# Middle tiles of an attention and MoE kernel: another order of the first layer's products, and q's main part turned right behind x

## The chip, the cores and the metric

The kernel runs on one core of a Trainium2 chip. A core has a matrix engine (PE, with its weight loads shown as PEld), a vector engine (DVE), a scalar engine (ACT), GpSimd (POOL), a queue engine for transfers (SP), and 16 DMA engines. Each engine works through its own list of instructions; engines wait for one another through semaphores. The metric is the device time of one execution in microseconds, as a median of several runs; lower is better.

## What is computed

```python
kv  = np.einsum('bhsd,bhse->bhde', k, v)
out = np.einsum('bhsd,bhde->bhse', q, kv)
rms = np.sqrt(np.mean(out * out, axis=-1, keepdims=True) + 1e-06)
out = out / rms * g_norm
x = out.transpose(0, 2, 1, 3).reshape(B * S, H * D)
h = x @ w_in
g = h * (1.0 / (1.0 + np.exp(-1.702 * h)))
return g @ w_out
```

There are 8 batches with 8 heads, 576 rows and a head size of 64; x is 4608 x 512, w_in is 512 x 2048 and w_out is 2048 x 512. The output is float32. The kernel computes in float16 with float32 sums.

## The kernel before

**Tiles.** Of each batch's 576 rows, 512 make one tile (t = 0 to 7) and the 64 that remain are gathered from all batches into a ninth (t = 8). A tile passes through two layers. While a tile t is in its second layer, the attention of batch b = t + 1 runs between its matmuls, so that the next tile's x is ready when the first layer of t + 1 begins.

**Products.** From t = 1 on both layers use a seven-product scheme (Strassen's, in Winograd's form): a 2 x 2 block product takes seven block products and some sums. In the first layer (class `SevenIn`) the 16 column blocks of w_in form four parts, g = 0 to 3, each with seven products, p = 1 to 7. A step such as "25" is product 5 of part 2: four matmuls of 128 x 256. Products 1 and 2 take their moving operand from the first column half of x (the blocks b11 and b21); product 3 takes b22; products 5, 6, 7 and 4 take the sums t0, t1, t2 and t3, which DVE forms from x (`Sums.form`, L505 to L509). form(0) is b12 - b11 and form(1) is b22 + t0, so both need the second column half of x.

**Evacuation of a product.** Each part has banks x, y and z in PSUM. Product 1 goes to x; bank x is then copied to y (`copy(self.snap[1], ...)`, L587), and product 6 accumulates on x. Product 5 goes to z, and z is copied to the SBUF tile s5 (L589). When both 5 and 6 are done, DVE writes x + s5 into z (L591), on which product 3 then accumulates. Product 2 accumulates on y. Behind product 7 DVE adds x into s5 (L593). Products 2, 3, 4 and 7 return a gate: an ACT activation (L557) that writes gT. `hid_seven` (L733) walks the steps; the gate of a step is emitted behind the product, and the copy, of the next step. A step's number is its place in the list, and the dictionaries of the plan name such places.

**The plan.** `LATER` (L941) is used for t = 2 to 6. In it `{1: 'DAAA', 5: 'AAAD'}` gives, for parts 0 to 3, the engine of the copy behind product 1 and behind product 5: D is DVE and A is ACT. The string "aooa" gives the pools of the banks x, "aahh" those of z; y is always in h. Pool o has two buffers, which the second layer uses too: its bank z, then its bank x, whose last content is copied out by ACT at the tile's end (`place`, L677). `(0, 1, 5, 10)` are the steps behind which form(0) to form(3) are emitted. `{15: '34'}` puts one product behind matmul 15 of the second layer.

**The second layer and the attention in it.** `Seven.run` (L687) makes 112 matmuls in the order of products 1, 5, 6, 2, 7, 3, 4. Work put there by `at2(n, ...)` is emitted behind matmul n. The attention's `rows` come at 15, and `turn` at 35, 38, 46 and 48. A turn with an odd number issues on SP a DMA_TRANSPOSE (L365) of half of the normalised rows x16 into x, so at 38 the first and at 48 the second column half. The store of the first output half (L843) is issued behind matmul 95, the second at the end.

**Queues of transfers.** At 100 comes `transpose_q` of batch t + 2 (t = 1 to 5): two DMA_TRANSPOSE on SP, the main part into qTd (L289, one buffer, read by the next tile's `rows`) and the remaining rows into qTr (L291). SP's list in a tile is thus x's two halves, the first store, q's main part, q's rest, the second store. On POOL stand, in this order, the k load of batch t + 3 (at 15, behind the products that read k), a mark that waits for x (`after_turn`, L127), the v load and both remainders, a mark that waits for qTd (`after_queries`, L131), and the q load of batch t + 3 (L143, L149).

Of the kernel before, what the change touches and what calls it, by code (L numbers as in the profile page):

```python
# [16 lines left out]
def kernel(  # L17
# [119 lines left out]
    def q_rows(b):  # L137

        rows = qbuf if b % 2 else qraw.rearrange("p c x -> p (c x)")
        return rows[:, 0 : H * J * D]  # L140
# [79 lines left out]
    class Attention:  # L220
# [66 lines left out]
        def transpose_q(self):  # L287
            self.qTd = attn.tile([P, H * J // 2, P], F16, name="qTd", tag="qTd", bufs=1)
            nc.sync.dma_start_transpose(out=self.qTd, in_=q_rows(self.b))  # L289
            self.qTr = attn.tile([P, 2, P], F16, name="qTr", tag="qTr", bufs=1)  # L290
            nc.sync.dma_start_transpose(  # L291
                out=self.qTr, in_=qrem[self.b % 2].rearrange("p c e -> p (c e)")
            )
# [4 lines left out]
        def product(self, t, c):  # L298
            nc.tensor.matmul(t, self.kb[:, c, :], self.qT[c][:, 0:SM], start=True, stop=True)  # L299
# [226 lines left out]
    def copy(engine, to, src):  # L526
        (nc.vector.tensor_copy if engine == "D" else nc.scalar.copy)(to, src)  # L527

    class SevenIn:


        def __init__(self, hid, xs, g, todo):
            self.snap = {p: e[g] for p, e in todo.snap.items()}
            self.pool = todo.pool[g]
            self.gT, self.xs, self.g, self.i = hid.gT, xs, g, PARTS[g]
            self.bank, self.done = {}, set()
            self.s5 = stage.tile([P, 2, TH], F32, name="s5", tag="s5")
# [28 lines left out]
        def product(self, p):  # L566

            name = {1: "x", 6: "x", 7: "x", 4: "x", 2: "y", 5: "z", 3: "z"}[p]  # L570
            if p in (1, 5):
                self.open(name)
            bank = self.bank
            for a in range(2):
                for k in range(KH):
                    w, x = self.operands(p, a, k)
                    nc.tensor.matmul(  # L577
                        bank[name][:, a],
                        w,
                        x,  # L580
                        start=(p in (1, 5) and a == 0 and k == 0),
                        stop=(k == KH - 1),
                        skip_group_check=True,
                    )
            self.done.add(p)
            if p == 1:
                copy(self.snap[1], self.open("y"), bank["x"])  # L587
            elif p == 5:
                copy(self.snap[5], self.s5, bank["z"])  # L589
            if p in (5, 6) and self.done >= {5, 6}:  # L590
                nc.vector.tensor_add(bank["z"], bank["x"], self.s5)  # L591
            elif p == 7:
                nc.vector.tensor_add(self.s5, bank["x"], self.s5)  # L593
                return lambda: self.gate(1, 1, self.s5)
            elif p in (2, 3, 4):
                r, n = {2: (0, 0), 3: (0, 1), 4: (1, 0)}[p]
                return lambda: self.gate(r, n, bank[name])
# [312 lines left out]
    for fo in COLS[4:GROUP]:  # L910
# [28 lines left out]
        {'rows': (19, 19), 'add_up': (22, 26, 27, 31), 'table': 26, 'roots': (27, 33), 'turn': (40, 50, 51, 52)},  # L939
    )  # L940
    LATER = Plan(  # L941
# [4 lines left out]
        {1: 'DAAA', 5: 'AAAD'},  # L946
        "D",
        "aooa",
        "aahh",
        {15: '34'},  # L950
        (0, 1, 5, 10),
        {'rows': (15, 15), 'add_up': (17, 20, 24, 28), 'table': 24, 'roots': (28, 29), 'turn': (35, 38, 46, 48)},
    )
    LAST_TWO = Plan(
# [12 lines left out]
    def plan(t):  # L967
        return SECOND if t < EARLY else LATER if t < B - 1 else LAST_TWO
# [7 lines left out]
    for t in range(NT):  # L976
        b = t + 1
        u1, u2 = {}, {}

        def at1(i, f, *args):  # L980
            u1.setdefault(i, []).append(lambda: f(*args))

        def at2(i, f, *args):
            u2.setdefault(i, []).append(lambda: f(*args))  # L984

        def of(b, name, *args):
            return lambda: getattr(live[b], name)(*args)

        if t == 0:
            for l in range(2):  # L990
                at1(6, nc.vector.memset, kvd[l], 0.0)
            at1(7, of(0, "out", NPAIR))
            at1(7, scale_w_in, 0, 4)
            at1(7, w_in_sums, 0, 2)
            at1(8, start, 1)
            at1(12, scale_w_in, 4, 6)
            at1(12, w_in_sums, 2, 3)
            at1(13, load_q, 2)
            at2(4, setattr, a0, "ss_pool", Attention.ss_pool)
            at2(4, of(0, "ss", NPAIR, True))  # L1000
            at2(4, of(0, "apply", NPAIR))
            at2(18, weight_sum, 0, 0, HF)
            at2(18, scale_w_in, 6, 8)
            at2(18, w_in_sums, 3, 4)
            for c in range(NPAIR):
                at1(12, of(1, "pack_q", c))
                at2(9 + 3 * c, of(1, "q", c))
                at2((36, 36, 49, 49)[c], of(1, "kv", c))
                at2((41, 43, 54, 55)[c], of(1, "out", c))
                at2((45, 50, 58, 60)[c], of(1, "ss", c))  # L1010
                at2((48, 52, 58, 62)[c], of(1, "apply", c))
            for n in range(1, 4):
                at2(19, weight_sum, n, 0, 4)
                at2(38, weight_sum, n, 4, 6)
            at2(39, load_kv, 2, 0, H // 2, False)
            at2(51, clear_rest)
            at2(51, load_kv, 2, H // 2, H)

            def first_sum():
                made[1] = Sums(1, xT[1])  # L1020
                made[1].form(0)

            at2(55, first_sum)
        elif b < B:
            todo = plan(t)
            at = todo.attn
            if t == 1:
                at1(todo.steps.index("kv"), of(b, "kv_all", "D"))
                at1(5, start, b)
                at1(5, of(b, "transpose_q"))  # L1030
                at1(4, nc.scalar.preload_act_table_set, "gelu_apprx_sigmoid_and_others")
                for n, i in ((1, 8), (2, 11), (3, 16)):
                    at1(i, weight_sum, n, 6, HF)
                at1(22, load_kv, 3)
                at1(22, load_q, 3)
                at2(88, start, 3)
                at2(88, of(3, "kv_all", "A"))
                at2(89, load_kv, 4)
                at2(89, load_q, 4)
            elif t + 2 < B:  # L1040
                at2(at["rows"][0], start, t + 2)
                at2(at["rows"][0], of(t + 2, "kv_products"))
                at2(52, of(t + 2, "kv_copies", "A"))
                if t + 3 < B:
                    at2(at["rows"][0], load_kv, t + 3, 0, H, False, "k")
                    at2(101, after_turn, b)
                    at2(101, load_kv, t + 3, 0, H, True, "v")
                    at2(101, after_queries, t + 2)
                    at2(101, load_q, t + 3)
            if t + 2 < B:  # L1050
                at2(100, of(t + 2, "transpose_q"))
            at2(at["table"], nc.scalar.preload_act_table_set, "abs_reciprocal_sqrt_and_small")
            for h in range(2):
                at2(at["roots"][h], of(b, "roots", h))
            for j in range(J):
                if j < J // 2:
                    at2(at["rows"][j], of(b, "rows", j))
                for name in ("add_up", "turn"):
                    at2(at[name][j], of(b, name, j))
            rest = (80, 90, 96, 97) if 1 < t < B - 2 else (46, 74, 80, 82)  # L1060
            at2(rest[0], of(b, "out", NPAIR))
            at2(rest[1], of(b, "ss", NPAIR))
            at2(rest[2], of(b, "apply", NPAIR))
            at2(rest[3], nc.scalar.preload_act_table_set, "gelu_apprx_sigmoid_and_others")
        elif t < B:
            for name in ("ss_pool", "rest_pool"):
                at2(16, setattr, live[1], name, (ps_a, "att"))
            at2(16, of(1, "out", NPAIR))
            at2(34, nc.scalar.preload_act_table_set, "abs_reciprocal_sqrt_and_small")
            at2(44, of(1, "ss", NPAIR))  # L1070
            at2(50, of(1, "apply", NPAIR))
            at2(52, nc.scalar.preload_act_table_set, "gelu_apprx_sigmoid_and_others")
        layers(t, u1, u2)
# [30 lines left out]
```

## Time and profile before

| what | value |
|---|---|
| median of 3 runs | 258.92 us (258.73 to 259.25) |
| the profiled execution's own time | 259.85 us |
| its span, first to last instruction | 258.1 us |
| PE's granted clock | 1.000 |
| start of the first layer's matmuls of t = 2, 3, 4, 5, 6, 7 (us in the span) | 74.04, 100.25, 126.37, 153.60, 179.72, 205.10 |

In the profile a row of the timeline gives start and length in us, the engine, the line of the kernel, the operation, its tiles (output <- inputs), the count of merged instructions, and in brackets the idle time before it with what ended that. "h" stands for a bank of the first layer, "s" for s5, "o" for a bank of the second layer, "xS" for a formed sum. A row of waits gives the total in us, the number of waits, and the longest. A row of stretches gives the window, its length, each engine's busy time with its count of instructions (PE, PEld, DVE, ACT, POOL), PE's clock, the DMA share and GB/s. Matmuls overlap: a row's length reaches to the modelled end of its last one, so the rate is read from start to start.

### The profile page before, as it was taken

Reading aid. Unit: us, or ns where it says so; the run is one execution under the profiler, and the core shown is the slowest. Engines: PE = TensorE matmul, PEld = TensorE weight load, DVE = VectorE, ACT = ScalarE, POOL = GpSimd, SP = SyncE. Lnnn points to the kernel's source line nnn. Section 1 sums busy time; section 2 is a strip of 40 time slices with the busy share of each in tenths; the row PEclk is TensorE's granted clock in tenths of the full one; section 3 lists DMA queues with packets and bytes.
Section 4 is the critical chain, followed back from the end, with each engine's and each line's share of the span. In section 5 each row is a group of like instructions: output and inputs, shape, how many; then the busy total and the mean of one; then the engine's idle time right before and its main releaser. Section 6 shows DMA issues by size and latency. Waiting matters only on the chain.

```text
span 258.1 us, 6355 instructions
## 1 busy us (share of the span) xinstructions
PE 250.8 (97%) x2596; PEld 204.0 (79%) x2596; DVE 190.1 (74%) x339; ACT 180.2 (70%) x327; POOL 57.2 (22%) x91
## 2 busy tenths in 40 slices
PE   8889999999999999999899999999999999999994
PEld 2444554788888888888788888898888888888883
DVE  1565677899938794889469867986799787857872
ACT  3477725988769886988589958995899469536800
POOL 8872235116080103041160130200000000000013
PEclk9999999999999999999999999999999999999999
DMA  7999999999999986999999669986700430012005
GB/s 173 193 200 205 204 204 197 234 198 150 159 178 201 203 118 139 139 136 169 182 144 205 82 152 134 156 95 137 204 3 0 84 163 3 0 60 105 3 19 145
DMA packets 68671, 35.33 MB, mean 137 GB/s; under 512 B 37954, under 2 KB 66242, under 8 KB 68386
## 3 DMA queue, kind: packets, MB, share of 16 engines
q0 software_dynamic: 37616, 18.31, 55.6%
q1 hardware_dynamic: 30624, 16.29, 29.5%
q8 instruction: 20, 0.33, 0.5%
q10 hardware_dynamic: 402, 0.33, 0.4%
q14 instruction: 9, 0.07, 0.1%
HBM read 36.70 MB, written 9.44 MB: 179 GB/s over the span
## 4 chain that ended last, share of the span: by engine, by line
PE 89%; DMA 7%; DVE 1%; issue 0%; ACT 0%; POOL 0%; DVEq 0%
PE h L577 38%; PE o L697 36%; PE o L812 5%; PE hT L470 5%; DMA xT<-x 2%; DMA vbuf<-in_v_dram 2%; DMA qraw<-in_q_dram 2%; PE kvp L246 2%; PE outR L329 1%; PE ss L376 1%; DVE x L359 1%; PE outT L299 0%; PE q L451 0%; PE kvp L258 0%; DVE xT L386 0%
## 5 line engine op out<-in xcount | busy, mean ns | idle before, releaser
L557 ACT ACTIVATE gT<-h 128x512 f16<-128x512 f32 x96 | 52.3, 601 | 5.6 <-PE h L577 5.6
L577 PEld LDWEIGHTS <-ws 128*128 128x128 f16 x512 | 50.1, 98 | 7.0 <-issue 1.1
L577 PE MATMUL h<-xS,ws 128*128 128x256 f16 x384 | 53.0, 273 | 1.0 <-DVE xS L509 1.0
L697 PEld LDWEIGHTS <-gS 128*128 128x128 f16 x512 | 49.0, 98 | 6.2 <-DVE gS L629 0.3
L697 PE MATMUL o<-tw,gS 128*128 128x256 f16 x384 | 45.6, 273 | 0.0
L577 PEld LDWEIGHTS <-w_in_sb 128*128 128x128 f16 x384 | 37.5, 98 | 4.7
L697 PEld LDWEIGHTS <-gT 128*128 128x128 f16 x384 | 37.6, 98 | 4.3
L577 PE MATMUL h<-xT,w_in_sb 128*128 128x256 f16 x224 | 31.8, 273 | 0.0
L697 PE MATMUL o<-w_out_sb,gT 128*128 128x256 f16 x256 | 31.4, 273 | 0.0
L591 DVE TENSOR_TENSOR h<-h,s 128x512 f32<-128x512 f32 x32 | 22.3, 699 | 11.3 <-PE h L577 5.3
L674 DVE TENSOR_TENSOR osb<-o,qf 128x512 f32<-128x512 f32 (+1 forms) x25 | 16.7, 668 | 11.7 <-PE o L697 11.7
L593 DVE TENSOR_TENSOR s<-h,s 128x512 f32<-128x512 f32 x32 | 22.1, 691 | 4.4 <-PE h L577 3.3
L629 DVE TENSOR_TENSOR gS<-gT 128x512 f16<-128x512 f16 (+2 forms) x32 | 21.3, 685 | 0.6 <-ACT gT L557 0.6
L557 ACT ACTIVATE gT<-s 128x512 f16<-128x512 f32 x32 | 19.8, 628 | 2.6 <-DVE s L593 2.6
L731 POOL DMA_DIRECT2D out_dram<-osb x6 | 3.2, 540 | 82.5 <-DVE osb L674 82.5
L577 PE MATMUL h<-xS,w_in_sb 128*128 128x256 f16 x128 | 18.9, 272 | 0.0
L345 DVE TENSOR_REDUCE sum<-sq 128x8 f32<-128x512 f16 x24 | 14.9, 678 | 4.8 <-ACT sq L339 4.8
L984 ACT ACT_TABLE_LOAD x14 | 18.0, 1283 | 0.3
L317 ACT ACTIVATE sq<-outT 128x512 f16<-128x512 f32 (+1 forms) x16 | 7.8, 489 | 14.5 <-PE outT L299 8.9
L378 ACT ACTIVATE rs<-ss,eps_t 128x512 f32<-128x512 f32 (+1 forms) x16 | 9.2, 581 | 11.5 <-PE ss L376 11.4
L527 ACT COPY h<-h 128x512 f32<-128x512 f32 x27 | 15.4, 577 | 2.2 <-PE h L577 2.0
L577 PE MATMUL h<-xT,ws 128*128 128x256 f16 x112 | 16.8, 273 | 0.0
(104 smaller groups left out, 358.9 us busy)
## 6 DMA issues: line engine op xcount, KB each, us to landing
out_dram<-osb SPq DMA_DIRECT2D x8, 512.0 KB, 4.3
kraw<-in_k_dram POOLq DMA_DIRECT2D x5, 512.0 KB, 7.4
vbuf<-in_v_dram POOLq DMA_DIRECT2D x5, 512.0 KB, 10.2
out_dram<-osb SPq DMA_DIRECT2D x2, 1024.0 KB, 4.8
qraw<-in_q_dram POOLq DMA_DIRECT2D x3, 512.0 KB, 12.2
qbuf<-in_q_dram POOLq DMA_DIRECT2D x3, 512.0 KB, 6.0
out_dram<-osb SPq DMA_DIRECT2D x6, 192.0 KB, 5.7
w_in_sb<-in_moe_w_in_dram POOLq DMA_DIRECT2D x2, 512.0 KB, 9.8
```

Of the source, the lines that this page charges most:

```text
L345: nc.vector.tensor_reduce(out=self.sum4[:, j, :], in_=self.o[j][1].rearrange("p (x d) -> p x d", d=D), op=ALU.add, axis=mybir.AxisListType.X,)
L470: nc.tensor.matmul(self.h[fo], w_in_sb[:, ko, fo * P : (fo + 1) * P], self.x[:, ko], start=(ko == 0), stop=(ko == KO - 1),)
L527: (nc.vector.tensor_copy if engine == "D" else nc.scalar.copy)(to, src)
L557: nc.scalar.activation(self.gT[:, to, n * TH : (n + 1) * TH], src, AFT.Gelu_apprx_sigmoid)
L577: nc.tensor.matmul(bank[name][:, a], w, x, start=(p in (1, 5) and a == 0 and k == 0), stop=(k == KH - 1), skip_group_check=True,)
L591: nc.vector.tensor_add(bank["z"], bank["x"], self.s5)
L593: nc.vector.tensor_add(self.s5, bank["x"], self.s5)
L629: op(s[:, n, lo], a, b)
L674: nc.vector.tensor_add(o, ps, self.kept[with_][:, m])
L697: nc.tensor.matmul(o, a, w, start=(p in (1, 2, 5) and i == 0 and (mo == 0 or split)), stop=(i == HF - 1), skip_group_check=True,)
L812: nc.tensor.matmul(os[mo], gT[:, fo, mo * P : (mo + 1) * P], w_out_sb[:, fo, :], start=(fo == 0), stop=(fo == FO - 1),)
L984: u2.setdefault(i, []).append(lambda: f(*args))
```

## The change

In `LATER` the step "11" moves from the seventh to the third place, "22" and "25" change places, and a new step "10" stands behind "06". A part that has such a step "g0" is held: its product 1 is not followed by the copy of bank x into y, and the copy is emitted at step "10". form(0) and form(1) are both emitted behind step 0; the other numbers move by one with the longer list. `transpose_q` is split: q's main part is issued at matmul 49 of the second layer, directly behind x's second half, for t = 2 to 5 (at 100 as before for t = 1), and q's rest stays at 100.

```diff
         def transpose_q(self):
             self.qTd = attn.tile([P, H * J // 2, P], F16, name="qTd", tag="qTd", bufs=1)
             nc.sync.dma_start_transpose(out=self.qTd, in_=q_rows(self.b))
+
+        def transpose_rest(self):
             self.qTr = attn.tile([P, 2, P], F16, name="qTr", tag="qTr", bufs=1)
...
             self.snap = {p: e[g] for p, e in todo.snap.items()}
+            self.held = f"{g}0" in todo.steps
...
+            bank = self.bank
+            if p == 0:
+                copy(self.snap[1], self.open("y"), bank["x"])
+                return None
             name = {1: "x", 6: "x", 7: "x", 4: "x", 2: "y", 5: "z", 3: "z"}[p]
             if p in (1, 5):
                 self.open(name)
-            bank = self.bank
...
-            if p == 1:
+            if p == 1 and not self.held:
                 copy(self.snap[1], self.open("y"), bank["x"])
...
     LATER = Plan(
-        "21 01 25 22 05 06 11 02 15 26 03 16 12"
+        "21 01 11 22 25 05 06 10 02 15 26 03 16 12"
         " 07 31 27 13 17 35 36 04 23 24 32 33 14 37",
-        {22: ((0, 4, 0), (0, 4, 1)), 25: ((4, 6, 0),)},
+        {23: ((0, 4, 0), (0, 4, 1)), 26: ((4, 6, 0),)},
...
-        (0, 1, 5, 10),
+        (0, 0, 6, 11),
...
                 at1(5, of(b, "transpose_q"))
+                at1(5, of(b, "transpose_rest"))
...
             if t + 2 < B:
-                at2(100, of(t + 2, "transpose_q"))
+                at2(49 if t > 1 else 100, of(t + 2, "transpose_q"))
+                at2(100, of(t + 2, "transpose_rest"))
```

## The prediction

> **What bounds the kernel now.** I read the page first, then the chain of waits, then PE's waits, then a table of time by tile.
>
> ```profile
> span 258.1 us, 6355 instructions
> PE 250.8 (97%) x2596; PEld 204.0 (79%) x2596; DVE 190.1 (74%) x339; ACT 180.2 (70%) x327; POOL 57.2 (22%) x91
> ...
> PE 89%; DMA 7%; DVE 1%; issue 0%; ACT 0%; POOL 0%; DVEq 0%
> ```
>
> PE is 97% busy and 89% of the chain that ended last. So a change of order can gain only where PE stands idle. From the second tile on, PE's waits show one such place:
>
> ```profile
> PE h L577 <- DVE xS L509: 1.0, 1, 1.0
> ```
>
> The table of stretches, cut at the first L577 matmul of tiles t=4, 5 and 6, gives the price of that wait:
>
> ```profile
> 126.37:153.60 27.23, 26.27 (x303) 23.27 (x301) 20.66 (x35) 21.17 (x40) 6.92 (x11) 1.00 0.96 146
> 153.60:179.72 26.12, 26.12 (x303) 23.27 (x301) 20.33 (x34) 21.17 (x40) 3.72 (x7) 1.00 0.95 133
> ```
>
> Both tiles have 303 matmuls at clock 1.00; the fourth is 27.23 - 26.12 = 1.11 us longer. This is all that the change can win on PE. The timeline there (PE, then DVE, then SP's queue) shows why:
>
> ```profile
> 126.37 1.04 PE L577 MATMUL h<-xT,w_in_sb 128*128 128x256 f16 x8
> 128.37 0.60 PE L577 MATMUL h<-xS,ws 128*128 128x256 f16 x4 [0.96 <-DVE xS L509]
> ```
> ```profile
> 127.89 0.42 DVE L509 TENSOR_TENSOR xS<-xT 128x512 f16<-128x512 f16 x1 [2.04 <-DMA xT<-x]
> ```
> ```profile
> 120.56 3.70 SPq L365 DMA_TRANSPOSE xT<-x  x2
> ```
>
> Products 21 and 01 run, then 25 needs form(0), and form(0) needs x's second turned half, which landed late. DMA issues in the two stretches 120-124 and 142-150 us show how late: 5.9 us to landing, against 3.2 us one tile on.
>
> ```profile
> xT<-x SPq DMA_TRANSPOSE x2, 5.9
> ```
> ```profile
> xT<-x SPq DMA_TRANSPOSE x2, 3.2
> ```
>
> **The change, part by part.** No instruction is added or taken away. Three orders change in tiles t=2 to 6 (plan LATER): PE's products, with them ACT's and DVE's queues, and SP's queue.
>
> *Products.* I use the undisturbed tile t=5, which starts at 153.60. PE:
>
> ```profile
> 153.60 1.04 PE L577 MATMUL h<-xT,w_in_sb 128*128 128x256 f16 x8
> 154.47 0.60 PE L577 MATMUL h<-xS,ws 128*128 128x256 f16 x4
> 154.93 0.60 PE L577 MATMUL h<-xT,w_in_sb 128*128 128x256 f16 x4
> 155.36 1.04 PE L577 MATMUL h<-xS,ws 128*128 128x256 f16 x8
> 156.23 1.04 PE L577 MATMUL h<-xT,w_in_sb 128*128 128x256 f16 x8
> 157.11 1.04 PE L577 MATMUL h<-xS,ws 128*128 128x256 f16 x8
> 157.98 0.60 PE L577 MATMUL h<-xT,ws 128*128 128x256 f16 x4
> ```
>
> Four matmuls are a product. The rows are 21 and 01; 25; 22; 05 and 06; 11 and 02; 15 and 26; 03. The eleventh product (03) starts 4.38 us after the first, so a product takes 0.438 us. ACT and DVE beside it:
>
> ```profile
> 153.80 0.58 ACT L677 COPY osb<-o 128x512 f32<-128x512 f32 x1 [0.52 <-PE o L697]
> 154.28 0.59 ACT L527 COPY h<-h 128x512 f32<-128x512 f32 x1
> 155.11 0.58 ACT L527 COPY s<-h 128x512 f32<-128x512 f32 x1 [0.24 <-PE h L577]
> 156.00 0.58 ACT L527 COPY s<-h 128x512 f32<-128x512 f32 x1 [0.30 <-PE h L577]
> 156.48 0.60 ACT L557 ACTIVATE gT<-h 128x512 f16<-128x512 f32 x1
> 157.12 0.57 ACT L527 COPY h<-h 128x512 f32<-128x512 f32 x1
> ```
> ```profile
> 153.00 0.42 DVE L509 TENSOR_TENSOR xS<-xT 128x512 f16<-128x512 f16 x1
> 154.68 0.70 DVE L527 COPY h<-h 128x512 f32<-128x512 f32 x1 [1.26 <-PE h L577]
> 155.28 0.41 DVE L509 TENSOR_TENSOR xS<-xT,xS 128x512 f16<-128x512 f16 x1
> 156.61 0.70 DVE L591 TENSOR_TENSOR h<-h,s 128x512 f32<-128x512 f32 x1 [0.92 <-ACT s L527]
> ```
>
> ACT's rows are: the previous tile's last output copy; 21's copy; 25's copy to s5; 05's copy to s5; 22's gate; 11's copy. DVE's are form(0), 01's copy, form(1), and the add behind 06 (L591), which writes bank z of part 0. Product 03 accumulates into that bank, so it waits for this add, and the add for 05's copy.
>
> Durations: from a product's start to its copy 0.64 (154.47 to 155.11, 155.36 to 156.00); on ACT copy to gate 0.48 (156.00 to 156.48), gate to copy 0.64 (156.48 to 157.12; 11 had started at 156.23 and was ready at 156.87, so the engine set this); end of 05's copy to the add 0.03 (156.58 to 156.61); end of a DVE result to PE 0.06 (127.89 + 0.42 to 128.37).
>
> Before: the add ends at 157.31, so z is ready at 157.37, 0.61 us ahead of 03.
>
> After: 25 is the fifth product and no longer the third. It starts at 153.60 + 4 x 0.438 = 155.35, its copy at 155.99. The gate of 22, now one step ahead of 25, is queued right behind 25's copy and **ahead** of 05's copy (a step's gate is called behind the next step's product): 156.47. Then 05's copy 157.11 to 157.69, the add 157.72 to 158.42, z ready 158.48. 03 is still the eleventh product and wanted at 157.98: **PE waits 0.50 us.** 05's copy starts 1.11 us later than before (157.11 against 156.00); 0.61 of that was slack. ACT meanwhile stands idle between 154.87 and 155.99.
>
> The ACT row itself bears on this order: 22 started at 154.93, ready at 155.57, and ACT stood idle for 0.30 us before 156.00, yet the gate ran behind 05's copy. The Trainium skill's "PSUM — Partial Sum Buffer", section Engine vs sequencer instructions, says that ScalarE's and VectorE's queues are strictly first in, first out; the trace agrees with this 0.30 us. By that rule the wait is the 0.50; without it, with ACT free to choose, it would be gone.
>
> How often: all five tiles have this same chain. The waits of DVE in 74 to 206 us:
>
> ```profile
> DVE h L591 <- ACT s L527: 4.9, 5, 1.2
> ```
>
> Five waits, one a tile: +2.50 us. Bounds: if a copy can follow a gate after 0.48, 0.34 a tile; if each ACT instruction runs serially (0.58 + 0.60 in place of 0.48 + 0.64), and product 11, now third, waits 0.10 besides, 0.66 a tile. Product 11 takes the bank that the output copy at 153.80 frees at 154.38; with 0.06 that is 154.44 against a start at 154.48, so I take nothing for it. The range for five is 1.7 to 3.3, and I take 2.50 since each term is a row of the same tile. Behind 03 everything only shifts; PE is dense there and nothing takes the 0.50 back.
>
> *The forms.* form(0) and form(1) now both come ahead of 01's copy. With x in time they run at 153.00 to 153.83, before that copy is ready (154.68): nothing. 06 needs 01's copy (ends 155.38) at 156.23: covered. 11's copy, held back two products, lands behind 05's on ACT at 157.59 to 158.16; 16, wanted at 158.42, is covered.
>
> *q's main part.* Its DMA_TRANSPOSE moves ahead of the first store on SP, in t=2 to 5:
>
> ```profile
> 152.77 0.33 SPq L843 DMA_DIRECT2D out_dram<-osb  x1
> 153.28 5.50 SPq L289 DMA_TRANSPOSE qTd<-qraw  x1
> ```
>
> The store goes later by up to those 5.5 us. Its output tile has two buffers and is refilled two tiles on, so nobody waits. qTd is read in the next tile's rows, 15 us on. On POOL the mark for qTd stands ahead of the q load, the remainder loads and the next k load:
>
> ```profile
> 152.31 0.18 POOL L127 COPY mark<-xT 1x1 f16<-1x1 f16 x1 [8.76 <-DMA xT<-x]
> ...
> 154.31 0.70 POOL L120 DMA_DIRECT2D vbuf<-in_v_dram  x1
> 165.71 0.18 POOL L131 COPY mark<-qTd 1x1 f16<-1x1 f16 x1 [10.70 <-DMA qTd<-qraw]
> ```
>
> It waited 10.70 us; now q's load follows the v loads nearly at once. In t=3 the same wait had pushed the q load to 114.06, and the k load queues behind it:
>
> ```profile
> 114.06 0.89 POOL L143 DMA_DIRECT2D qbuf<-in_q_dram  x1
> ```
>
> These two ran into x's transposition at 120.56, the late one. With q loaded several us sooner, I take the 3.2 us landing there: -1.11 us (bounds 0 and -1.11). The Trainium skill's "DMA: Bandwidth & Descriptors", section Queues, rings and completion order, has each DMA engine alternate between queue rows packet by packet, and consume one ring in order. By it POOL's loads slow x and q's transposition behind x does not; the 5.9 against 3.2 us agrees, and the sum would be the same.
>
> The earlier q load stands behind v in POOL's queue. v's last piece and its reader:
>
> ```profile
> vbuf<-in_v_dram POOLq DMA_DIRECT2D x1, 64.0 KB, 11.1
> ```
> ```profile
> 167.68 0.82 PE L246 MATMUL kvp<-vbuf,kraw 128*64 128x64 f16 x40
> ```
>
> 154.31 + 11.1 = 165.4: 2.3 us of cover. I cost it at nothing; without that cover PE waits the excess.
>
> *Sum.* +2.50 - 1.11 = +1.39 us. The profiled execution took 259.85 us (span 258.1 and 1.75 around it), giving 261.24. The median of the runs, 258.92, is 0.93 lower, so 258.92 + 1.39 = **260.3 us**.
>
> **The rivals.**
> (a) *Only the gain.* 05's copy reaches DVE early enough that 03 doesn't wait, and x's stall goes: 258.92 - 1.11 = 257.8, faster. It decides at a copy start of 156.61 or sooner, 0.50 ahead of my 157.11. For it: ACT is only 70% busy. Against it: its queue order, and the same chain in five tiles.
> (b) *Nothing to win.* In unprofiled runs, 0.93 us shorter, x may land in time already. Then only the waits remain: 258.92 + 2.50 = 261.4.
> (c) *x stays late* in t=3 (landing 127.8, form(0) 127.89): 25 starts at 128.37 against 128.12, and 03 is 0.75 us late in all against 1.11 before. Four tiles at 0.50 and -0.36: +1.64, 260.6.
> (d) *q's transposition slows x.* If the two share the engines and 3.2 us doubles, x lands at 152.31 + 3.2 = 155.5; form(0) and 0.06 more make 25 start at 156.0, 0.65 late, which adds to the 0.50. Four tiles: +2.6, 262.9. It decides only from a landing after 154.87, 2.5 us later than now; x standing ahead in the same queue speaks against it.
> (e) *The waits are short* (0.2 a tile): +1.0 - 1.11, no change, 258.8.
>
> **How the numbers follow.** My forecast 0.64, (a) 0.13, (b) 0.12, (c) 0.03, (d) 0.03, (e) 0.05. A measurement here tells 0.2%, 0.5 us, from no change. The forecast's own range is 1.7 to 3.3 less 1.11: 259.5 to 261.1. With (b) and (c) and the runs' spread (258.73 to 259.25) the range is 259.3 to 261.6, leaving out (a), (d) and (e), 0.21. Slower 0.82, within 0.05, faster 0.13.
>
> **What would show it.** Right: PE h L577 waits five times, some 0.5 us each, for DVE h L591; its wait for xS is gone; 22's gate stands between 25's and 05's copies on ACT; POOL's mark for qTd waits far less than 10 us, and x lands in about 3.2 us in t=3. Wrong: no wait of PE at 03 (a), five tiles of equal length as before but one shorter; or waits for xS or kvp that weren't there (d).

## The result, and the profile after

| | before | after |
|---|---|---|
| median | 259.25 us (11 runs, 258.73 to 260.3) | 260.51 us (11 runs, 260.11 to 262.3) |
| ratio after / before | | 1.0063, 95% interval 1.0047 to 1.0079 |
| span of the profiled execution | 258.1 us | 258.4 us |

The changed kernel is slower by some 0.5 to 0.8%. The prediction was 260.3 us, in a range of 259.3 to 261.6. The two profiled spans are much closer together than the medians. That has a reason, which the experiments give: the profiled execution of before holds a wait that a second profile of the same kernel doesn't have.

The lines of the changed kernel are shifted: L509 is now L511, L527 is L529, L557 is L560, L577 is L583, L591 is L597, L674 is L680, L677 is L683, L697 is L703. Its page, the span, PE's row and the chain:

```profile
span 258.4 us, 6349 instructions
...
PE 250.2 (97%) x2596; PEld 203.5 (79%) x2596; DVE 190.2 (74%) x339; ACT 179.0 (69%) x327; POOL 56.6 (22%) x91
...
PE 88%; DMA 4%; ACT 3%; DVE 2%; issue 0%; POOL 0%
```

ACT and DVE have entered the chain with 3% and 2%. PE's waits (total, times, longest) name where:

```profile
PE h L583 <- DVE h L597: 1.0, 5, 0.2
```

These are five waits for the add behind 06, one a tile; the wait for the formed sum xS is gone. The 1.0 us understates the loss, since this view counts from the modelled end of the last matmul and not from the next start. The stretches of t = 2 to 6, each from its first matmul to that of the next tile, give it (window, length, then the engines' busy times):

```profile
73.79:100.28 26.49, 26.29 (x304) 23.27 (x302) 20.09 (x34) 20.94 (x40) 4.92 (x8) 1.00 1.13 170
100.28:126.76 26.48, 26.28 (x303) 23.26 (x301) 20.34 (x35) 20.93 (x40) 5.18 (x10) 1.00 1.00 149
126.76:153.25 26.49, 26.29 (x304) 23.27 (x301) 20.35 (x35) 20.93 (x40) 5.92 (x10) 1.00 1.03 152
153.25:179.74 26.49, 26.29 (x304) 23.25 (x302) 20.11 (x34) 20.93 (x40) 3.90 (x7) 1.00 0.92 127
179.74:205.47 25.73, 25.53 (x264) 22.53 (x261) 21.05 (x37) 19.36 (x36) 0.00 (x0) 1.00 0.31 75
```

The first four take 26.48 or 26.49 us where an undisturbed tile of before took 26.12: 0.37 us a tile. The fifth, t = 6, has fewer matmuls and takes 25.73 us against 25.37 in the second profile of before. In all this is 1.83 us. The timelines of ACT, DVE and PE at the start of t = 5, now at 153.25:

```profile
153.93 0.59 ACT L529 COPY h<-h 128x512 f32<-128x512 f32 x1
155.65 0.58 ACT L529 COPY s<-h 128x512 f32<-128x512 f32 x1 [1.12 <-PE h L583]
156.13 0.60 ACT L560 ACTIVATE gT<-h 128x512 f16<-128x512 f32 x1
156.62 0.59 ACT L529 COPY s<-h 128x512 f32<-128x512 f32 x1
157.08 0.62 ACT L529 COPY h<-h 128x512 f32<-128x512 f32 x1
```
```profile
157.24 0.70 DVE L597 TENSOR_TENSOR h<-h,s 128x512 f32<-128x512 f32 x1 [2.22 <-ACT s L529]
```
```profile
156.75 1.04 PE L583 MATMUL h<-xS,ws 128*128 128x256 f16 x8
157.99 0.60 PE L583 MATMUL h<-xT,ws 128*128 128x256 f16 x4 [0.20 <-DVE h L597]
```

ACT's order is 21's copy, 25's copy, 22's gate, 05's copy, 11's copy. It idles 1.12 us before 25's copy, the gate takes its turn, and 05's copy starts 3.37 us into the tile (156.62 - 153.25), where it was 2.40 before (156.00 - 153.60). DVE's add waits 2.22 us for it. Product 03 starts at 157.99 in place of 156.75 + 8 x 0.109 = 157.62.

q's main part goes as the change says. SP's queue and POOL's mark for qTd in the same tile turn:

```profile
147.43 2.61 SPq L367 DMA_TRANSPOSE xT<-x  x2
150.22 1.88 SPq L289 DMA_TRANSPOSE qTd<-qraw  x1
152.42 0.76 SPq L849 DMA_DIRECT2D out_dram<-osb  x1
```
```profile
154.84 0.18 POOL L131 COPY mark<-qTd 1x1 f16<-1x1 f16 x1
155.11 0.89 POOL L143 DMA_DIRECT2D qbuf<-in_q_dram  x1
```

The mark no longer waits, and q's load is issued at 155.11 where it was at 166.16.

### The profile page after: what moved, and what is told of

It reads as the page before. It is cut to its first block, busy times and chain, and to the rows that moved or that the text cites. A ratio compares the mean times of both kernels' runs of the same rounds, so it can differ in the third digit from the quotient of the medians.

```text
span 258.4 us, 6349 instructions
## 1 busy us (share of the span) xinstructions
PE 250.2 (97%) x2596; PEld 203.5 (79%) x2596; DVE 190.2 (74%) x339; ACT 179.0 (69%) x327; POOL 56.6 (22%) x91
## 4 chain that ended last, share of the span: by engine, by line
PE 88%; DMA 4%; ACT 3%; DVE 2%; issue 0%; POOL 0%
PE o L703 38%; PE h L583 34%; PE o L818 5%; PE hT L472 5%; DMA vbuf<-in_v_dram 2%; ACT s L529 2%; DMA qraw<-in_q_dram 2%; PE kvp L246 2%; DVE h L597 1%; PE outR L331 1%; ACT gT L560 1%; PE ss L378 1%; PE outT L301 0%; PE q L453 0%; PE kvp L258 0%
## 5 line engine op out<-in xcount | busy, mean ns | idle before, releaser
L560 ACT ACTIVATE gT<-h 128x512 f16<-128x512 f32 x96 | 52.6, 602 | 6.2 <-PE h L583 6.2
L583 PEld LDWEIGHTS <-ws 128*128 128x128 f16 x512 | 50.0, 98 | 7.7 <-issue 1.9
L703 PEld LDWEIGHTS <-gS 128*128 128x128 f16 x512 | 49.0, 98 | 6.2 <-DVE gS L635 0.3
L583 PE MATMUL h<-xS,ws 128*128 128x256 f16 x384 | 52.2, 273 | 0.0
L703 PE MATMUL o<-tw,gS 128*128 128x256 f16 x384 | 45.6, 273 | 0.0
L583 PEld LDWEIGHTS <-w_in_sb 128*128 128x128 f16 x384 | 37.4, 98 | 4.8
L703 PEld LDWEIGHTS <-gT 128*128 128x128 f16 x384 | 37.6, 98 | 4.3
L597 DVE TENSOR_TENSOR h<-h,s 128x512 f32<-128x512 f32 x32 | 22.2, 697 | 14.8 <-ACT s L529 11.1
L703 PE MATMUL o<-w_out_sb,gT 128*128 128x256 f16 x256 | 31.4, 273 | 0.0
L583 PE MATMUL h<-xT,w_in_sb 128*128 128x256 f16 x224 | 31.1, 273 | 0.0
L680 DVE TENSOR_TENSOR osb<-o,qf 128x512 f32<-128x512 f32 (+1 forms) x25 | 16.7, 668 | 11.8 <-PE o L703 11.7
L560 ACT ACTIVATE gT<-s 128x512 f16<-128x512 f32 x32 | 19.9, 628 | 2.6 <-DVE s L599 2.6
L583 PE MATMUL h<-xS,w_in_sb 128*128 128x256 f16 x128 | 18.9, 273 | 0.0
L115 POOL DMA_DIRECT2D kraw<-in_k_dram x7 | 6.0, 853 | 57.9 <-PE kvp L246 53.6
L583 PE MATMUL h<-xT,ws 128*128 128x256 f16 x112 | 16.8, 272 | 1.0 <-DVE h L597 1.0
```

Of the source, the lines that this page charges most:

```text
L560: nc.scalar.activation(self.gT[:, to, n * TH : (n + 1) * TH], src, AFT.Gelu_apprx_sigmoid)
L583: nc.tensor.matmul(bank[name][:, a], w, x, start=(p in (1, 5) and a == 0 and k == 0), stop=(k == KH - 1), skip_group_check=True,)
L680: nc.vector.tensor_add(o, ps, self.kept[with_][:, m])
L703: nc.tensor.matmul(o, a, w, start=(p in (1, 2, 5) and i == 0 and (mo == 0 or split)), stop=(i == HF - 1), skip_group_check=True,)
```

## The experiments

Theory 1 was that the loss is product 03's wait behind ACT's queue. The rivals were the moved transposition, DVE's own queue, and another wait under the same name. Medians of before beside each experiment: 258.93 us (35 runs) for the first four, 259.07 and 259.15 (13 runs each) for the later ones.

**The order alone.** q's main part goes back to matmul 100.

```diff
-                at2(49 if t > 1 else 100, of(t + 2, "transpose_q"))
+                at2(100, of(t + 2, "transpose_q"))
```

> The new product order alone; q's main part is turned at matmul 100 again, behind the first store. Theory 1 (the loss is product 03's wait for the add behind ACT's queue): five waits of PE for DVE's add, 0.37 us each from start to start as in the changed kernel (1.83 us in all); in t=3 x's second half may land late as before, and then 25 starts 0.25 us late and 03 about 0.6 us late in all. Time 260.5 to 261.0 us. Theory 2 (the moved transposition costs the time, by the store or POOL's queue behind it): no slower than before, 259.3 or less.

Measured: 260.66 us, ratio 1.0060 (1.0038 to 1.0081). All five waits are there at full size:

```profile
PE h L583 <- DVE h L597: 1.0, 5, 0.2
```

The x of t = 3 landed in 3.95 us and cost nothing. The order alone gives the whole loss.

**q alone.** The plan's steps, ready and sums as before, with the transposition at 49.

```diff
-        "21 01 11 22 25 05 06 10 02 15 26 03 16 12"
+        "21 01 25 22 05 06 11 02 15 26 03 16 12"
...
-        (0, 0, 6, 11),
+        (0, 1, 5, 10),
```

> q's main part turned right behind x alone; the old product order. Theory 1: no wait of PE for DVE's add; no wait for form(0), since q's load no longer stands in front of the k load when x is turned in t=3 (x lands in about 3.2 us, the tile takes 26.12 us and not 27.23): 258.3 to 258.8 us against 259.25 before. Theory 2: slower than before, about 260.5. Rival 3 (the late x is chance and not q's load): the wait for form(0) is there in some tile, about 259.3.

Measured: 259.04 us, ratio 1.0007 (0.9983 to 1.0032). So the move costs nothing, but it doesn't win what was expected either; of the three expectations rival 3 came nearest. x's second half took 4.9 us in t = 3, though q's load had long been done; PE lost 0.08 us there (the tile took 26.20 us). So x can be late in t = 3 without q's load.

**05's copy on DVE.**

```diff
-        {1: 'DAAA', 5: 'AAAD'},
+        {1: 'DAAA', 5: 'DAAD'},
```

> The changed kernel with the copy behind product 05 on DVE in place of ACT, so that it isn't queued behind 22's gate. Theory 1: the copy starts 2.84 us into the tile on DVE, the add 3.45, z is ready at 4.2, before product 03 at 4.38: no wait of PE there, 1.83 us less than the changed kernel, 258.5 to 258.9 us. A rival (DVE itself is full there, by both forms ahead of the copies): PE still waits about 0.3 us in each of five tiles, 260.2 or more.

Measured: 259.06 us, ratio 0.9997 (0.9975 to 1.0018). No wait of PE for the add is left, and the tiles t = 2 to 5 take 26.12 or 26.13 us each. So DVE is not the limit. The time is that of before and not below it.

**22's gate one step later.** ACT's work is unchanged, and two instructions change places.

```diff
             behind, gates = gates, []
+            if step == "25" and "10" in todo.steps:
+                behind, gates = [], behind
```

> The changed kernel with 22's gate called one step later, behind 05's copy on ACT; nothing else. Theory 1: 05's copy starts 2.88 us into the tile (3.37 in the changed kernel), the add 3.50, z ready at 4.25, 03 at 4.38 without a wait: 258.6 to 259.0 us. Rival (PE waits for something else, the forms or the bank of 11): the 0.37 us stay, 260.5. It also tells what sets the 0.64 us between a gate and 11's copy in the kernel before: if the reuse of bank y (22's gate reads the bank that this copy fills), the copy comes 0.64 us behind the gate's start, at 4.00; if it is only the engine's pace of 0.49, at 3.85.

Measured: 259.11 us, ratio 0.9990 (0.9971 to 1.0009); this is 1.4 us less than the changed kernel's 260.51, and 1.55 us less than the 260.66 of the order alone, which ran beside it. ACT and DVE in t = 5, which starts at 152.36, and the stretch:

```profile
154.75 1.07 ACT L529 COPY s<-h 128x512 f32<-128x512 f32 x2 [1.12 <-PE h L583]
155.71 0.62 ACT L560 ACTIVATE gT<-h 128x512 f16<-128x512 f32 x1
156.36 0.57 ACT L529 COPY h<-h 128x512 f32<-128x512 f32 x1
```
```profile
155.86 0.70 DVE L597 TENSOR_TENSOR h<-h,s 128x512 f32<-128x512 f32 x1 [1.73 <-ACT s L529]
```
```profile
152.36:178.48 26.12, 26.12 (x304) 23.27 (x301) 19.94 (x33) 20.90 (x40) 3.95 (x7) 1.00 0.88 123
```

The add starts 3.50 us into the tile, as expected, and the 0.37 us are gone. 11's copy comes at 156.36 - 152.36 = 4.00, 0.65 us behind the gate: the value expected from the reuse of bank y, and not the 3.85 of the engine's pace.

**Before, profiled again.** No edit.

> The kernel before, profiled once more. If x's late landing in t=3 belongs to the program, PE waits again about 1 us for form(0) at 25 (the tile 27.2 us); if it is chance, x lands in 3 to 5 us and all middle tiles take 26.1 to 26.2 us.

Measured: 258.62 us in one run, and no wait for form(0): the stretches that were 26.12, 27.23, 26.12 us are now 26.12, 26.13, 26.12.

```profile
126.24:152.37 26.13, 26.13 (x304) 23.28 (x302) 20.75 (x35) 21.17 (x40) 6.92 (x11) 1.00 1.00 152
```

x's second half took 4.6 us in t = 3 and arrived just soon enough. So the wait of 1.11 us doesn't come in every execution of this program.

**The order under a late x.** What does the new order do where x is late? The last turn was put later, first at matmul 70, in the old order, in the changed kernel, and in the changed kernel with the gate moved.

```diff
-        {'rows': (15, 15), 'add_up': (17, 20, 24, 28), 'table': 24, 'roots': (28, 29), 'turn': (35, 38, 46, 48)},
+        {'rows': (15, 15), 'add_up': (17, 20, 24, 28), 'table': 24, 'roots': (28, 29), 'turn': (35, 38, 46, 70)},
...
-                at2(49 if t > 1 else 100, of(t + 2, "transpose_q"))
+                at2(71 if t > 1 else 100, of(t + 2, "transpose_q"))
```

> The kernel before (old product order, q at 100) with the last turn of tiles t = 2 to 6 put at matmul 70 of the second layer in place of 48, so that x's second half lands some 2.4 us later in every tile, about 1.0 us into the next tile. Theory: the third product (25) needs form(0) at 0.87 and gets it at about 1.6, so PE waits some 0.7 us at 25 in each of t = 3 to 6 (t = 7 has another plan): 261.5 to 263 us. If x has more slack than that, no waits and 259.

> The changed kernel with the same late turn (q's main part at 71, behind it). Theory: 25 is the fifth product, wanted at 1.75, and form(0) is there at 1.6: no wait there; form(1) and 01's copy end at about 2.7, so 06 waits about 0.1 us; the 0.37 us at product 03 stay as they are. Less than the old order under the same late x: some 0.45 us a tile in t = 3 to 6 against 0.7.

> The changed kernel with 22's gate behind 05's copy, and the same late turn (q's main part at 71). Theory: no wait at 25 and none at 03, about 0.1 us a tile at 06: 2 us or more less than the old order under the same late x. That would show what the product order itself buys once the queue of ACT is mended.

Measured: 260.62, 261.73 and 260.95 us. Both comparisons missed what was expected: the changed kernel was 1.1 us slower than the old order and not faster, and with the gate moved it was 0.3 us slower and not 2 us faster. x was late in too few tiles to tell. Its second half was issued only some 2 us later and mostly still landed 0.2 to 0.5 us ahead of the tile; in the profiled executions t = 6 was late in all three kernels, t = 3 only in the two with the new order. The same again at matmul 90 (q at 91):

> The kernel before with the last turn of t = 2 to 6 at matmul 90 in place of 48 (70 was not late enough: x landed 0.3 to 0.5 us ahead of the tile). x's second half should land some 1.9 us into each tile; form(0) is then ready at 2.4, and 25, the third product, is wanted at 0.87: PE waits some 1.5 us in each of t = 3 to 7, 266 to 267 us in all.

> The changed kernel with 22's gate behind 05's copy, and the same last turn at 90 (q's main part at 91). Theory: 25 is wanted at 1.75, so it waits 0.7 us in t = 3 to 6, 06 nearly nothing more, 03 nothing; t = 7 has another plan and waits 1.5 us as in the old order: 263 to 264 us, some 3 us less than the old order under the same late x. If the new order buys nothing, the two are equal.

Measured: 265.44 us (ratio 1.0246, 1.0213 to 1.0278) in the old order, 262.74 (1.0140, 1.0108 to 1.0172) in the new one with the gate moved. Both stay a little under what was expected: x landed 0.9 to 1.6 us into the tiles t = 4 to 7 and not 1.9, and only in t = 3 later (2.4 and 2.5 us). The tiles t = 4 and 5, with x landing 0.9 us in (old) and 1.1 us in (new):

```profile
129.68:156.41 26.73, 26.26 (x303) 23.27 (x301) 20.33 (x34) 21.18 (x40) 5.90 (x9) 1.00 0.98 148
156.41:183.13 26.72, 26.27 (x303) 23.27 (x301) 20.32 (x34) 21.18 (x40) 4.99 (x8) 1.00 0.85 128
```
```profile
128.17:154.38 26.21, 26.21 (x304) 23.27 (x301) 20.43 (x34) 20.97 (x40) 5.88 (x9) 1.00 1.00 151
154.38:180.61 26.23, 26.23 (x304) 23.27 (x301) 20.43 (x34) 20.98 (x40) 4.97 (x8) 1.00 0.84 130
```

In these two tiles a late x costs 0.60 us each in the old order and 0.09 to 0.11 in the new one; in t = 3 it costs 2.08 us (28.20 us in all) and 1.55 (27.67). The two kernels also differ in q's place, which cost nothing by itself with x in time. The order has a use, then, where x is late. With x in time it wins nothing, and with 22's gate ahead of 05's copy it costs 0.37 us a tile.

**Moving the instruction fetches.** In the traces, x's slow landings had one thing in common: a 16 KB packet of the queue named instruction on one DMA engine while x was on its way. The queue's row in two windows of the kernel with the gate moved, around x's second half in t = 3 (landing 4.8 us; in t = 2, with 3.4 us, the queue has no row):

```profile
q8 instruction: 1, 0.02, 1.7%
...
xT<-x SPq DMA_TRANSPOSE x1, 4.8
```

The test adds 32 small matmuls ahead of the first ones, on a tile that nothing reads, which moves these packets.

```diff
+    for _ in range(32):
+        nc.tensor.matmul(idle_ps[:, 0:1], kvb[1][:, 0, :], kvb[1][:, 0, 0:1], start=True, stop=True)
     busy(12)
```

> The changed kernel with 22's gate behind 05's copy, and 32 more one-column matmuls at the very start, that change no result. They move the places at which PE's instructions are fetched (16 KB packets on the queue named instruction) by 64 instructions, some 3.5 us earlier in every tile. Theory (a slow landing of x is such a packet on one of the DMA engines while x is on its way): in t = 3 and t = 5 the packet now comes ahead of x's second half, which lands in about 3.2 us where it took 4.8 and 4.9; in t = 2 it comes some 1.7 us behind the issue, where there was none, and the landing of 3.35 us may grow to 4 to 5. Rival (the place in the kernel sets it, other loads or stores beside x): t = 3 and t = 5 stay at 4 to 5 us and t = 2 at 3.3.

Measured: 259.63 us, ratio 1.0016 (0.9990 to 1.0042). In t = 2, from 96 to 101 us, there is now such a packet, and x takes 4.9 us:

```profile
q8 instruction: 1, 0.02, 1.2%
...
xT<-x SPq DMA_TRANSPOSE x1, 4.9
```

In t = 3 (122.1 to 125.5 us) there is none, and x takes 3.3:

```profile
q1 hardware_dynamic: 2624, 0.66, 100.4%
issues: line engine op xcount, KB each, median us to landing
xT<-x SPq DMA_TRANSPOSE x1, 3.3
```

In t = 5 the expectation missed: the packet came 2.0 us behind the issue all the same (its place isn't a fixed number of instructions ahead of PE), and x took 5.4 us with it. In t = 6, which the expectation didn't name, packets now start 1.3 us behind the first half's issue and with the second half's, and the halves take 4.7 and 4.3 us; in the kernel with the gate moved they took 3.1 to 3.3. So the slow landing went where the packet went, in t = 2, 3 and 6, and stayed where it stayed.

## Why the prediction was right, point by point

- **Product 03's wait: right in place, cause and count; 0.37 us and not 0.50.** The failing step is "on ACT [...] gate to copy 0.64 (156.48 to 157.12; [...] so the engine set this)". In the changed kernel the copy of 05 follows the gate after 156.62 - 156.13 = 0.49 us, the same pace as a gate behind a copy. The 0.64 us of before belong to a wait of 11's copy: it fills bank y of part 1, which in the pool of three buffers takes the place of the bank that 22's gate reads. The kernel with the gate moved bears that out (4.00 us, not 3.85). It isn't that a copy into a bank of PSUM is slow to start: in the changed kernel 11's copy follows 05's after 157.08 - 156.62 = 0.46 us, with 22's gate done at 156.73. With 0.49 the prediction's own chain has z ready at 158.33 against 157.98, a wait of 0.35 us. Of the bounds given, the lower (0.34) was the right end. In all: 1.83 us and not 2.50.
- **x's stall, -1.11 us: not there in the usual execution.** The kernel before, profiled again, doesn't have it. Nor does the median: q alone, with 0.08 us of it in its trace, takes 1.0007 of before's time (0.9983 to 1.0032), where a gain of 1.11 us would be 0.9957. The rival "nothing to win" had this right. The failing step is the one that priced the gain at what one execution lost, and laid x's lateness on the q load ("With q loaded several us sooner, I take the 3.2 us landing there"). With q early, x's second half in t = 3 took 3.6 us in the changed kernel and 4.9 with q alone. What made the 5.9 us of the first profile stays open. q's load, issued at 114.06, landed in 6.0 us, ahead of x's first half at 120.56. k's load did run into x. Its rows in the first and the second profile of before:

```profile
kraw<-in_k_dram POOLq DMA_DIRECT2D x1, 512.0 KB, 8.3
```
```profile
kraw<-in_k_dram POOLq DMA_DIRECT2D x1, 512.0 KB, 6.4
```

Issued at 116.15 and 115.29, it landed at about 124.4 and 121.7, and x's second half was issued at 121.88 and 121.76. So it ran beside x for 2.5 us in the one and no longer in the other. The instruction packet of the first profile came only 3.4 us behind x's issue, when a usual landing of 3.0 to 3.4 us is over, too late to explain the delay by itself. But 4.6 to 4.9 us also came about without a load of POOL beside x, so the 5.9 against 3.2 us is not the plain sign of POOL's loads that the prediction took it for.
- **The two errors took each other's place, which is luck.** +2.50 - 1.11 was +1.39; the parts as measured are +1.83 and about 0 from the usual execution of before. The ratio of 1.0063 is 1.63 us of 259.25 (interval 1.2 to 2.0), which holds 1.83. The difference of the medians is 1.26. So the predicted time came within 0.2 us of the measured one by a wait that was priced 0.67 us too high and a gain of 1.11 us that is not usually there. The direction and the place of the loss are not luck: 1.83 us alone on the prediction's 258.92 gives 260.75, also slower and inside its range.
- **Nothing for the forms, for 11's copy and bank, for v's load and for the store behind q: right.** 11 starts third without a wait, PE's only waits in the changed kernel between 74 and 206 us are the five for the add, and q alone costs nothing (1.0007).
- **ACT's queue is in order: shown.** Two neighbours changing places on ACT take the whole wait away. The Trainium skill's "PSUM — Partial Sum Buffer", section Engine vs sequencer instructions, says strictly first in, first out; the 0.37 us that come and go with the gate's place agree with it.
- **q's transposition behind x does not slow x** by the doubling that rival (d) feared: with it, x takes 3.2 to 3.4 us in t = 2 and 4. The second half, directly ahead of q, takes some 0.2 us more than without it (3.3 to 3.4 against 3.1 to 3.2).

The rival (a), the gain alone, fell at the point it named: 05's copy starts 3.37 us into the tile, against the 3.01 us from which 03 would not wait. No kernel tried beats the one before; those without the wait are equal to it within the noise.

## What to carry to other kernels

When the order of one engine's work changes, write out the queues of the engines behind it again: here a gate and a copy changed places on ACT because a product moved by two steps, and the engine that was reordered paid 0.37 us a tile for it. A gap between two instructions is the engine's pace only if neither their inputs nor the buffer that the second one writes can have held it up. Before pricing a stall at what it cost in the one profile, ask whether it is in the other executions too; here a second profile of the same kernel was enough to show that it need not be.

## What the runs showed of the hardware that wasn't expected

Instructions arrive as DMA packets, and these can delay the transposition of x. The page of the changed kernel counts them among what the 16 DMA engines do:

```profile
q8 instruction: 20, 0.33, 0.5%
```

That is 16 KB a packet, each mostly 0.9 to 1.4 us long on one DMA engine. We take this queue to be PE's: 0.33 MB is 64 bytes for each of PE's 5192 matmuls and weight loads, and more PE instructions moved the packets. Of 117 of x's transpositions behind 85 us in the 13 profiles, 78 had no such packet starting between 0.9 us ahead of their issue and 3.0 behind it (limits drawn from these same traces); 76 of these landed in 3.0 to 3.4 us. The other two took 5.9 us, the stall in the first profile of before, and 4.1, with a packet 3.4 and 4.0 us behind the issue. Of the 39 with one, 20 took 3.6 to 5.4 us, and 19 landed as usual. Which of the 16 engines takes the packet, and whether that decides between the 20 and the 19, was not tried. The Trainium skill's "Runtime: NRT & Kernel Launch", section Instruction fetch mechanics, says that instruction memory is refilled in such blocks by the sequencer's own DMA queue and calls the cost mostly hidden. For PE itself the traces agree: in the kernel with the gate moved, the tiles t = 2 to 5 have two or three packets each, and take 26.12 or 26.13 us. But x, on its way beside such a packet, landed some 1.5 us later (4.9 against 3.4 us in t = 2, 4.8 against 3.3 in t = 3).
